# One core, decay attention feeding two expert layers: VectorE pinned in the first block, later attention twelve slots later

## The chip, the cores and the metric

One core of a Trainium2 chip runs the whole program once. The metric is the device time of that execution in microseconds (us). Engines: PE is TensorE, DVE VectorE, ACT ScalarE, POOL GpSimd, SP the queue that issues nearly all DMAs.

## What is computed

Cut from the reference (a batch of 4, 8 heads, 768 steps, head size 48):

```python
for t in range(S):                     # complex decay attention, one state per head
    new_re = ar * S_re - ai * S_im
    new_im = ar * S_im + ai * S_re
    S_re, S_im = new_re + k_t v_t, new_im
    y[t] = q_t @ S_re
x = y as (3072 tokens, 384)
h = x @ w_in                           # 384 to 2048
sp = log1p(exp(minimum(h, 20)))
x2 = (h * tanh(sp)) @ w_out            # 2048 to 384
out = (x2 @ w_a * (x2 @ w_b)) @ w2_out # 384 to 1536 to 384
```

## The kernel before

**Blocks, chunks, units.** The 768 steps are cut into six pieces of 128, and a chunk is one piece of one batch: 24 chunks, numbered 0 to 23, four of them (the four batches of one piece) make a block of 512 tokens. The first expert layer goes through six blocks, and in each through 16 units f of 128 columns of h. A unit computes `hps` (`moe1_h`, L544: nine matmuls, because f32 operands are split into a high and a low part), then on DVE and ACT the factor of the activation (`mish_factor`: the minimum of h on DVE at L550, then Exp, Square, Ln, Exp on ACT, each reading what the one before wrote), then on DVE the product with h (`mish_product`: L561 in the first block, which writes `gh`; L564 in the others), and two units later the matmuls of `moe1_x2` (L587) on that product. `hps` has two PSUM buffers in the first five blocks: the matmuls of unit f+2 wait until the product of unit f has read its `hps`. The second expert layer follows, 72 units of its own.

**Attention beside it.** The attention of chunks 0 to 3 is the lead-in, ahead of the first unit. Attention of chunks 4 to 23 runs beside the first layer in slots. A table (`early`, `late`) names the step and its slot relative to `slot_0(c)`; a new chunk starts every 8 slots. The steps that the prediction speaks of: `decay_1` to `decay_4` (Square on ACT; add on DVE, L250; Ln and Exp on ACT; DVE at L259, L265, L266, the first of which reads what Exp wrote), `angle` (Arctan on ACT), `carry` (DVE, L277), `split_ell` and `split_theta` (POOL L286, DVE L288 and L290, from chunk 8 on), the running sums on PE (`pl`, `pt`, L299), `reduce_angle` (DVE, L323 to L325), `trig` (two Sin on ACT), `rotate` (two DVE instructions of 128x768, L364, that read the sines), `transposes` (PE, copied out by ACT as `qT`, `kT`), `scores` (PE `psc`, DVE L399), `outer` (`pu`), `values` (`py`), `store_y2` (DVE `yl`, L440, then a DMA to memory) and `read_x` (the DMA that reads it back as `xh`, `xl`, the input of the next block's `hps`). ACT holds one table at a time: Exp and Ln need one, Sin and Arctan the other, and each change is an instruction of its own (L55).

**Weights.** In the first block each unit also takes a step of a loading pipeline (`do_w`): a 768 KB piece of the weights comes in as 64-bit words, three DVE instructions turn it into f32 (L166 to L168, tiles `wf` and `wout`), ACT copies the high part (`winh`, `wouth`) and POOL subtracts it (L178, `winl`, `woutl`).

**What sets the order.** The program is recorded in the order of the code, and a scheduler then chooses each engine's own order from its estimates, subject to the data. `in_order` and `behind` add artificial dependences: `in_order(first, engines)` makes each recorded instruction of an engine wait for the one recorded before it, so that the scheduler can't reorder them. Before, this is done for the lead-in alone. `run_to(n)` records the slots up to n; in a block with `base` to `want` slots, half of a unit's share comes ahead of the minimum of h (L550) and half ahead of the product. The first block runs to slot 46, where all of chunk 7 is done.

Of the kernel before, what the change touches and what calls it, by code (L numbers as in the profile page):

```python
# [21 lines left out]
def kernel(  # L22
# [27 lines left out]
    def act(**kw):  # L50


        name = TABLES.get(kw["func"])
        if name is not None and name != table["name"]:
            load = nc.scalar.preload_act_table_set(name)  # L55
            for y in table["ops"] + [table["last"]]:
                if y is not None:
                    follow(load, y)
            table.update(ops=[], last=load, name=name)
        x = nc.scalar.activation(**kw)  # L60
        if name is not None:
            follow(x, table["last"])
            table["ops"].append(x)

    B, H, S, D = q.shape
# [8 lines left out]
    NF = FF // P  # L74
# [125 lines left out]
    def w_cols(nm, f):  # L200
        return [w[:, :, f % 2 * P:(f % 2 + 1) * P] for w in weights[nm, f // 2]]
# [246 lines left out]
    def outer(c):  # L448
        if chunk(c)[0] == NC - 1:
            return  # L450
        kh, vt = st["kh", c], st["v", c]
        p = st["pu", c] = (ps_l if c < B else ps_a).tile([D2, H, D], F32, tag="pl" if c < B else "ps", name="pu")
        for h in range(H):
            nc.tensor.matmul(  # L454
                p[:, h, :], lhsT=kh[:, h].rearrange("p a d -> p (a d)"), rhs=vt[:, h * D:(h + 1) * D],
                start=True, stop=True,
            )

    def state(c):
        j, b = chunk(c)  # L460
        if j == NC - 1:
            return
        Wb = W[b][:D2, :H * D].rearrange("p (h d) -> p h d", d=D)
        us, g = st.pop(("pu", c)), st.pop(("g", c))
        if j:
            nc.vector.tensor_tensor(Wb, Wb, us, ALU.add)
            us = Wb
        (nc.gpsimd if us is Wb else nc.vector).tensor_tensor(Wb, us, g.to_broadcast([D2, H, D]), ALU.mult)
# [24 lines left out]
            nc.vector.tensor_tensor(xl, raw, xh.bitcast(F32), ALU.subtract)  # L493


    PERIOD = 8

    def slot_0(c):
        return PERIOD * (c - B)

    early = [
        (-5, load_a), (-1, decay_1), (0, decay_2), (0, decay_3), (1, tangent), (1, decay_4), (2, angle),
# [26 lines left out]
    def ready_slot(c):  # L529

        return slot_0(c) + late[-1][0] + 1
# [4 lines left out]
    def moe1_h(blk, f, pool):  # L536
        xh, xl = xh_t[blk], xl_t[blk]
        p = pool.tile([P, TN], F32, tag="ps" if pool is ps_a else "h", name="hps")
        hi, lo = w_cols("in", f)
        ops = []  # L540
        for kk in range(KM):
            ops += [(hi, xh, kk), (hi, xl, kk), (lo, xh, kk)]
        for i, (w, x, kk) in enumerate(ops):
            nc.tensor.matmul(p, lhsT=w[:, kk, :], rhs=x[:, kk, :], start=(i == 0), stop=(i == len(ops) - 1))  # L544
        return p

    def mish_factor(p):

        m = mp.tile([P, TN], F32, tag="m", name="m")
        nc.vector.tensor_scalar(m, p, 20.0, None, ALU.min)  # L550
        act(out=m, in_=m, func=AF.Exp)
        act(out=m, in_=m, func=AF.Square, bias=bias_one)
        act(out=m, in_=m, func=AF.Ln, scale=0.2, bias=bias_fifth)
        act(out=m, in_=m, func=AF.Exp, scale=-1.0)
        return m

    def mish_product(p, m, blk):

        if not blk:
            g = mp.tile([P, TN], F32R, tag="gh", name="gh").bitcast(F32)  # L560
            nc.vector.scalar_tensor_tensor(g, m, 2.5, p, ALU.subtract, ALU.mult)  # L561
            return [g]
        on_act = blk == NB - 1
        nc.vector.scalar_tensor_tensor(m, m, 2.5, p, ALU.subtract, ALU.mult)  # L564
        gh = mp.tile([P, TN], F32R, tag="gh", name="gh")
        gl = mp.tile([P, TN], F32R, tag="gl", name="gl")
        if on_act:
            act(out=gh, in_=m, func=AF.Copy)
        else:
            nc.vector.tensor_copy(gh, m)  # L570
        (nc.vector if on_act else nc.gpsimd).tensor_tensor(gl, m, gh.bitcast(F32), ALU.subtract)  # L571
        return gh, gl
# [157 lines left out]
    def run_to(n):  # L730
        while slot[0] < min(n, n_slots):
            attn_slot(slot[0])
            slot[0] += 1
# [23 lines left out]
    def do_w():  # L757
        next(weights1, None)
# [3 lines left out]
    def traced():  # L762
        return len(nc.cur_bb.bb.instructions)

    def in_order(first, engines):

        last = {}
        for x in nc.cur_bb.bb.instructions[first:]:
            if x.engine in engines:
                if x.engine in last:  # L770
                    tc.add_manual_dep(x, last[x.engine], no_sync, reason="lead")
                last[x.engine] = x.name
        return last

    def behind(first, last):
        for x in nc.cur_bb.bb.instructions[first:]:
            if x.engine in last:
                tc.add_manual_dep(x, last[x.engine], no_sync, reason="after the lead")
# [56 lines left out]
    E = mybir.EngineType  # L835
    first = traced()
    weights1 = lead_in()
    last, after_lead = in_order(first, (E.DVE, E.Activation, E.PE, E.Pool)), traced()
# [10 lines left out]
    def make_room():  # L849

        att.close()
        early.append(right.enter_context(tc.tile_pool(name="w2a", bufs=1, side="right")))
        spool.append(right.enter_context(tc.tile_pool(name="st2a", bufs=2, side="right")))
# [6 lines left out]
    ready, lag = {}, 2  # L860
    for ui in range(len(units) + lag):
        if ui == 3:
            behind(after_lead, last)
        if ui < len(units):
            blk, f = units[ui]
            if f == 0:
                base = slot[0]
                want = ends[blk + 1] if blk + 1 < NB else n_slots
                if blk == NB - 1:
                    make_room()  # L870
            p = moe1_h(blk, f, ps_a if blk == NB - 1 and f % 2 else ps_h)
            do_w()
            run_to(base + (want - base) * (2 * f + 1) // (2 * NF))
            m = mish_factor(p)
            if blk == 1 and f % 2 == 0:
                whole["out", f // 2][1]()
            if blk == NB - 1 and f % 5 != 4 or blk == NB - 2 and f >= NF - 2:
                next(prep, None)
        if ui == 1:
            for c in range(B):  # L880
                outer(c)
                state(c)
            tail.close()
            ps_x = w1.enter_context(tc.tile_pool(name="ps_x", bufs=1, space=PSUM))
            wps.append(allp.enter_context(tc.tile_pool(name="wp1", bufs=NF)))
        if ui >= lag:
            moe1_x2(*units[ui - lag], *ready.pop(ui - lag))
        if ui < len(units):
            run_to(base + (want - base) * (2 * f + 2) // (2 * NF))
            ready[ui] = mish_product(p, m, blk)  # L890

    w1.close()
    p2 = allp.enter_context(tc.tile_pool(name="p2", bufs=3))
# [210 lines left out]
```

## Time and profile before

| | us |
|---|---|
| three runs | 1108.72, 1111.19, 1113.58 (median 1111.19) |
| the profiled execution: its own time | 1108.67 |
| its span, first to last instruction | 1107.0 |
| PE busy | 1060.1 (96%) |
| DVE busy | 658.1 (59%) |
| ACT busy | 607.7 (55%) |
| POOL busy | 226.7 (20%) |

The profiled execution took 1108.67 us, of which 1107.0 are its span. The busy shares are averages over a lead-in, six blocks of the first layer and 72 units of the second; they say little of any one stage, so the stretches are asked for one at a time.

### The profile page before, as it was taken

Reading aid. Unit: us, or ns where it says so; the run is one execution under the profiler, and the core shown is the slowest. Engines: PE = TensorE matmul, PEld = TensorE weight load, DVE = VectorE, ACT = ScalarE, POOL = GpSimd, SP = SyncE. Lnnn points to the kernel's source line nnn. Section 1 sums busy time; section 2 is a strip of 40 time slices with the busy share of each in tenths; the row PEclk is TensorE's granted clock in tenths of the full one; section 3 lists DMA queues with packets and bytes.
Section 4 is the critical chain, followed back from the end, with each engine's and each line's share of the span. In section 5 each row is a group of like instructions: output and inputs, shape, how many; then the busy total and the mean of one; then the engine's idle time right before and its main releaser. Section 6 shows DMA issues by size and latency. Waiting matters only on the chain.

```text
span 1107.0 us, 15213 instructions
## 1 busy us (share of the span) xinstructions
PE 1060.1 (96%) x5740; PEld 882.8 (80%) x5740; DVE 658.1 (59%) x998; ACT 607.7 (55%) x962; POOL 226.7 (20%) x220
## 2 busy tenths in 40 slices
PE   3989989999999999999999999999999999999997
PEld 1856667888788788878877878888888888888886
DVE  4899995777777666777569998642322412322222
ACT  6669778888788787788757862221121222221211
POOL 2012163344333343343322122200000000000000
PEclk9999989999999999999999999999999999999999
DMA  9546754333444343334236366310010100100000
GB/s 201 107 123 172 191 142 96 95 65 72 96 85 86 81 94 65 65 74 98 65 91 200 123 196 215 104 57 1 21 38 1 43 15 1 43 1 1 29 1 31
DMA packets 203545, 90.87 MB, mean 82 GB/s; under 512 B 144781, under 2 KB 187850, under 8 KB 203466
## 3 DMA queue, kind: packets, MB, share of 16 engines
q1 hardware_dynamic: 203450, 89.82, 32.4%
q8 instruction: 47, 0.77, 0.3%
q14 instruction: 32, 0.26, 0.1%
q10 hardware_dynamic: 16, 0.01, 0.0%
HBM read 72.44 MB, written 17.36 MB: 81 GB/s over the span
## 4 chain that ended last, share of the span: by engine, by line
PE 73%; DVE 12%; ACT 8%; issue 4%; DMA 2%; POOL 0%; SPq 0%; ACTq 0%; DVEq 0%; POOLq 0%
PE ops L667 14%; PE psa L642 13%; PE psb L642 13%; PE hps L544 12%; PE x2ps L587 11%; ACT m L60 4%; PE psc L395 3%; PE py L419 2%; PE pu L454 2%; DVE m L550 2%; PE pqT L377 1%; PE pkT L377 1%; DVE m L564 1%; ACT s L60 1%; ACT L55 1%
## 5 line engine op out<-in xcount | busy, mean ns | idle before, releaser
L653 DVE TENSOR_TENSOR a_sb<-a_sb,psb 128x512 f32<-128x512 f32 x72 | 49.4, 686 | 224.5 <-PE psb L642 224.5
L60 ACT ACTIVATE m<-m 128x512 f32<-128x512 f32 x192 | 119.7, 627 | 81.3 <-DVE m L550 79.7
L60 ACT ACTIVATE ph<-a_sb 128x512 fp32r<-128x512 f32 x72 | 45.4, 631 | 156.9 <-DVE a_sb L653 156.9
L544 PE MATMUL hps<-xh,winh 128*128 128x512 f32 x288 | 120.3, 419 | 7.9 <-DVE gh L561 6.8
L60 ACT ACTIVATE a_sb<-psa 128x512 f32<-128x512 f32 x72 | 42.9, 596 | 153.9 <-PE psa L642 151.8
L571 POOL TENSOR_TENSOR gl<-m,gh 128x512 fp32r<-128x512 f32 x64 | 83.6, 1306 | 161.5 <-DVE gh L570 148.8
L544 PE MATMUL hps<-xl,winh 128*128 128x512 f32 x288 | 114.3, 397 | 0.4 <-DMA xl<-yt_dl 0.3
L544 PE MATMUL hps<-xh,winl 128*128 128x512 f32 x288 | 113.8, 395 | 0.0
L667 PE MATMUL ops<-woh,ph 128*128 128x384 f32 x288 | 97.3, 338 | 0.0
L667 PE MATMUL ops<-woh,pl 128*128 128x384 f32 x288 | 97.2, 338 | 0.0
L587 PE MATMUL x2ps<-gl,wouth 128*128 128x512 f32 x240 | 94.8, 395 | 2.2 <-DVE gl L571 1.1
L667 PE MATMUL ops<-wol,ph 128*128 128x384 f32 x288 | 96.8, 336 | 0.0
L587 PE MATMUL x2ps<-gh,wouth 128*128 128x512 f32 x240 | 93.9, 404 | 2.3 <-ACT gh L60 1.9
L587 PE MATMUL x2ps<-gh,woutl 128*128 128x512 f32 x240 | 93.8, 391 | 0.0
L642 PE MATMUL psa<-xh,wal 128*128 128x512 f32 x216 | 85.3, 395 | 0.0
L642 PE MATMUL psa<-xl,wah 128*128 128x512 f32 x216 | 85.2, 394 | 0.0
L642 PE MATMUL psa<-xh,wah 128*128 128x512 f32 x216 | 84.4, 391 | 0.0
L642 PE MATMUL psb<-xh,wbh 128*128 128x512 f32 x216 | 84.3, 390 | 0.0
L642 PE MATMUL psb<-xh,wbl 128*128 128x512 f32 x216 | 84.3, 390 | 0.0
L642 PE MATMUL psb<-xl,wbh 128*128 128x512 f32 x216 | 84.2, 390 | 0.0
L564 DVE SCALAR_TENSOR_TENSOR m<-m,hps 128x512 f32<-128x512 f32 x80 | 54.5, 683 | 37.1 <-ACT m L60 37.0
L655 DVE TENSOR_TENSOR pl<-a_sb,ph 128x512 fp32r<-128x512 f32 x72 | 52.3, 726 | 38.9 <-ACT ph L60 38.9
(143 smaller groups left out, 2349.0 us busy)
## 6 DMA issues: line engine op xcount, KB each, us to landing
wraw<-in_moe_w_out_dram SPq DMA_DIRECT2D x14, 768.0 KB
wraw<-in_moe_w_in_dram SPq DMA_DIRECT2D x8, 768.0 KB
a<-in_a_re_dram SPq DMA_DIRECT2D x24, 192.0 KB
a<-in_a_im_dram SPq DMA_DIRECT2D x24, 192.0 KB
q<-in_q_dram SPq DMA_DIRECT2D x24, 192.0 KB
k<-in_k_dram SPq DMA_DIRECT2D x24, 192.0 KB
v<-in_v_dram SPq DMA_DIRECT2D x24, 192.0 KB
wraw<-in_moe_w_a_dram SPq DMA_DIRECT2D x6, 768.0 KB
```

The lines of the kernel that those rows point to most:

```text
L60: x = nc.scalar.activation(**kw)
L377: nc.tensor.transpose(p[:, i, :], src[:, hf * HH + i].rearrange("p a d -> p (a d)"), ident)
L395: nc.tensor.matmul(p[:, i, :], lhsT=st["kT", c, hf][:, i, :], rhs=st["qT", c, hf][:, i, :], start=True, stop=True)
L419: nc.tensor.matmul(p[par * 64:(par + 1) * 64, i, :], lhsT=w[:, col:col + 64], rhs=x[:, first + par, :], start=(n == 0), stop=(n == len(ter ...
L544: nc.tensor.matmul(p, lhsT=w[:, kk, :], rhs=x[:, kk, :], start=(i == 0), stop=(i == len(ops) - 1))
L564: nc.vector.scalar_tensor_tensor(m, m, 2.5, p, ALU.subtract, ALU.mult)
L571: (nc.vector if on_act else nc.gpsimd).tensor_tensor(gl, m, gh.bitcast(F32), ALU.subtract)
L587: nc.tensor.matmul(x2ps[m], lhsT=w[:, ms], rhs=x, start=(f == 0 and i == 0), stop=(f == NF - 1 and i == len(terms) - 1),)
L642: nc.tensor.matmul(p, lhsT=w[:, kk, :], rhs=x[:, kk, :], start=(i == 0), stop=(i == len(ops) - 1))
L653: nc.vector.tensor_tensor(a_sb, a_sb, pb, ALU.mult)
L655: nc.vector.tensor_tensor(lo, a_sb, hi.bitcast(F32), ALU.subtract)
L667: nc.tensor.matmul(ops_t[t], lhsT=x[:, tsl], rhs=w, start=(f == 0 and i == 0), stop=(f == NF2 - 1 and i == 2),)
```

## The change

Three things. In the first block the minimum of h is recorded right after a unit's `hps`, ahead of the weight step and the slots, and the product ahead of `moe1_x2` and of the second half of the slots; the other blocks keep their code. When the 16 units of the first block are recorded, DVE is pinned to the recorded order from the lead-in's end to that point. And `slot_0` of chunks 8 to 23 is 12 slots higher, so that the second block has 44 slots (46 to 90) instead of 32 and the blocks after it 32 as before.

```diff
-    PERIOD = 8
+    PERIOD, REST = 8, 12
 
     def slot_0(c):
-        return PERIOD * (c - B)
+
+        return PERIOD * (c - B) + (REST if c >= 2 * B else 0)
...
     for ui in range(len(units) + lag):
         if ui == 3:
             behind(after_lead, last)
+        if ui == NF:
+            in_order(after_lead, (E.DVE,))
...
             p = moe1_h(blk, f, ps_a if blk == NB - 1 and f % 2 else ps_h)
+            if not blk:
+                m = mish_factor(p)
             do_w()
             run_to(base + (want - base) * (2 * f + 1) // (2 * NF))
-            m = mish_factor(p)
+            if blk:
+                m = mish_factor(p)
+            else:
+                ready[ui] = mish_product(p, m, blk)
...
             run_to(base + (want - base) * (2 * f + 2) // (2 * NF))
-            ready[ui] = mish_product(p, m, blk)
+            if blk:
+                ready[ui] = mish_product(p, m, blk)
```

DVE in the first block, before, from the minimum of unit 2 on (numbers tell the buffers apart; `m_793` is unit 3):

```order
L550 TENSOR_SCALAR m_748<-hps_724 128x512
L250 TENSOR_TENSOR s_746<-s_746 128x384
L166 TENSOR_SCALAR wf32_780<-wraw_649 128x768
L550 TENSOR_SCALAR m_793<-hps_770 128x512
L167 SCALAR_TENSOR_TENSOR wf32_780<-wraw_649,wf32_780 128x768
L168 SCALAR_TENSOR_TENSOR wf32_780<-wraw_649,wf32_780 128x768
L259 TENSOR_TENSOR a_630<-a_630,r_762 128x384
L265 TENSOR_SCALAR s_746<-s_746 128x384
L561 SCALAR_TENSOR_TENSOR gh_768<-m_748,hps_724 128x512
```

The same place now, unit 3 whole (`m_780` to the minimum of unit 4, `m_832`), behind the end of unit 2:

```order
L562 SCALAR_TENSOR_TENSOR gh_754<-m_734,hps_724 128x512
L250 TENSOR_TENSOR s_752<-s_752 128x384
L259 TENSOR_TENSOR a_631<-a_631,r_764 128x384
L265 TENSOR_SCALAR s_752<-s_752 128x384
L266 SCALAR_TENSOR_TENSOR size_767<-r_764,s_752 128x384
L551 TENSOR_SCALAR m_780<-hps_770 128x512
L166 TENSOR_SCALAR wf32_786<-wraw_655 128x768
L167 SCALAR_TENSOR_TENSOR wf32_786<-wraw_655,wf32_786 128x768
L168 SCALAR_TENSOR_TENSOR wf32_786<-wraw_655,wf32_786 128x768
L562 SCALAR_TENSOR_TENSOR gh_799<-m_780,hps_770 128x512
L364 TENSOR_TENSOR qh_807<-q_661,a_202 128x768
L364 TENSOR_TENSOR kh_809<-k_663,a_202 128x768
```

Every unit now reads minimum, three decode instructions, product, attention. Work that stood between L250 and its reader L259 stands elsewhere, and no minimum comes ahead of the product before it.

ACT beside it now, from the last step of unit 3's factor to the first of unit 4's:

```order
L60 ACTIVATE m_780<-m_780 128x512
L55 ACT_TABLE_LOAD
L60 ACTIVATE a_202<-a_202 128x384
L60 ACTIVATE a_202<-a_202,bias_hpi_68 128x384
L60 ACTIVATE a_631<-a_631 128x384
L55 ACT_TABLE_LOAD
L60 ACTIVATE winh3_839<-wf32_786 128x768
L60 ACTIVATE qT0_128<-pqT_849 96x512
L60 ACTIVATE kT_860<-pkT_855 96x512
L60 ACTIVATE m_832<-m_832 128x512
```

The pair of sines `a_202` that L364 reads stands behind unit 3's factor and a table change, and unit 4's factor behind two changes, three activations and three copies.

PE at the seam of the first two blocks, before (`gh_1600` is unit 14's product, `hps_1676` the first unit of the second block):

```order
L377 MATMUL pkT_1662<-ident_61,kh_1622 96x128 x4
L587 MATMUL x2ps0_754<-gh_1600,wout7_1412 128x512
L587 MATMUL x2ps1_756<-gh_1600,wout7_1412 128x512
L299 MATMUL pt_1669<-sh_1645,csum_r_63 128x384
L299 MATMUL pt_1669<-sl_1646,csum_r_63 128x384
L377 MATMUL pqT_1686<-ident_61,qh_1620 96x128 x4
L377 MATMUL pkT_1692<-ident_61,kh_1622 96x128 x4
L587 MATMUL x2ps2_758<-gh_1600,wout7_1412 128x512
L544 MATMUL hps_1676<-xh_1023,winh0_275 128x512
```

The sums and transposes there belong to chunks 8 and 9, and the second block's first unit needs the product of unit 14.

The same place now (`hps_1542` is unit 15, `hps_1580` and `hps_1618` are the first two of the second block, `gh_1565` is unit 15's product):

```order
L545 MATMUL hps_1542<-xh_455,winl7_1402 128x512
L588 MATMUL x2ps0_756<-gh_1470,wout6_1262 128x512
L588 MATMUL x2ps1_758<-gh_1470,wout6_1262 128x512
L588 MATMUL x2ps2_760<-gh_1470,wout6_1262 128x512
L588 MATMUL x2ps0_756<-gh_1515,wout7_1405 128x512
L588 MATMUL x2ps1_758<-gh_1515,wout7_1405 128x512
L588 MATMUL x2ps2_760<-gh_1515,wout7_1405 128x512
L588 MATMUL x2ps0_756<-gh_1565,wout7_1405 128x512
L545 MATMUL hps_1580<-xh_1024,winh0_275 128x512
L545 MATMUL hps_1618<-xh_1024,winh0_275 128x512
```

The attention work is gone from the seam, and the second block's first matmul now stands behind the product of unit 15, the last of the first block.

## Rows read from the trace of the kernel before

**Rows 1.** The page, busy time and share of the span by engine.

```profile
PE 1060.1 (96%) x5740; PEld 882.8 (80%) x5740; DVE 658.1 (59%) x998; ACT 607.7 (55%) x962; POOL 226.7 (20%) x220
```

**Rows 2.** Stretches, first and second block: busy us (count) per engine, clock, DMA.

```profile
58.40:187.80 129.40, 119.12 (x648) 83.37 (x647) 113.67 (x163) 102.09 (x158) 40.80 (x30) 0.96 0.60 154
187.80:284.70 96.90, 96.39 (x607) 79.87 (x605) 69.71 (x110) 78.08 (x122) 37.01 (x39) 1.00 0.36 77
```

**Rows 3.** Timeline, DVE, first block: start us, length us, what, [idle before].

```profile
59.21 0.55 DVE L166 TENSOR_SCALAR wout<-wraw 128x768 uint32<-128x768 uint32 x1
59.68 0.95 DVE L167 SCALAR_TENSOR_TENSOR wf<-wraw,wf 128x768 uint32<-128x768 uint32 x1
62.28 0.95 DVE L168 SCALAR_TENSOR_TENSOR wout<-wraw,wout 128x768 uint32<-128x768 uint32 x1
63.15 0.69 DVE L550 TENSOR_SCALAR m<-hps 128x512 f32<-128x512 f32 x1
...
148.04 0.68 DVE L550 TENSOR_SCALAR m<-hps 128x512 f32<-128x512 f32 x1
...
181.56 0.68 DVE L550 TENSOR_SCALAR m<-hps 128x512 f32<-128x512 f32 x1
```

**Rows 4.** Stretch from the first unit to unit 11's minimum, columns as in 2.

```profile
58.40:148.00 89.60, 82.22 (x445) 57.60 (x444) 83.55 (x120) 70.08 (x107) 24.02 (x16) 0.98 0.62 166
```

**Rows 5.** Timeline, DVE and ACT, unit 6's minimum, factor and product.

```profile
105.20 0.68 DVE L550 TENSOR_SCALAR m<-hps 128x512 f32<-128x512 f32 x1
105.92 0.63 ACT L60 ACTIVATE m<-m 128x512 f32<-128x512 f32 x1 [0.91 <-DVE m L550]
...
108.09 0.63 ACT L60 ACTIVATE m<-m 128x512 f32<-128x512 f32 x1
...
108.76 0.69 DVE L561 SCALAR_TENSOR_TENSOR gh<-m,hps 128x512 f32<-128x512 f32 x1
```

**Rows 6.** Timeline, ACT, a change of tables and back.

```profile
123.32 0.63 ACT L60 ACTIVATE m<-m 128x512 f32<-128x512 f32 x1
123.97 1.28 ACT L55 ACT_TABLE_LOAD   x1
125.26 0.52 ACT L60 ACTIVATE a<-a 128x384 f32<-128x384 f32 x1
...
127.20 1.28 ACT L55 ACT_TABLE_LOAD   x1
```

**Rows 7.** Timeline, DVE and ACT, the sum of decay_2 and its Ln and Exp.

```profile
118.03 0.55 DVE L250 TENSOR_TENSOR s<-s 128x384 f32<-128x384 f32 x1
118.62 0.85 ACT L60 ACTIVATE s<-s 128x768 f32<-128x768 f32 x1 [2.03 <-DVE s L250]
119.50 0.85 ACT L60 ACTIVATE r<-s 128x768 f32<-128x768 f32 x1
```

**Rows 8.** Timeline, POOL and DVE, weight split and decode side by side.

```profile
63.75 1.80 DVE L277 SCALAR_TENSOR_TENSOR a<-size,a 1x384 f32<-1x384 f32 x1
...
142.97 6.83 POOL L178 TENSOR_TENSOR woutl<-wout,wouth 128x768 fp32r<-128x768 f32 x3 [0.34 <-ACT wouth L60]
...
145.67 2.44 DVE L167 SCALAR_TENSOR_TENSOR wout<-wraw,wout 128x768 uint32<-128x768 uint32 x1
```

**Rows 9.** Timeline, DVE and PE, the store of y and the third block's first units.

```profile
279.27 0.68 DVE L440 TENSOR_TENSOR yl<-py,yh 128x512 fp32r<-128x512 f32 x1
...
286.29 0.50 PE L544 MATMUL hps<-xl,winh 128*128 128x512 f32 x1 [0.29 <-DMA xl<-yt_dl]
```

**Rows 10.** Timeline, PE, first and third unit of the second block.

```profile
187.75 0.79 PE L544 MATMUL hps<-xh,winh 128*128 128x512 f32 x1
188.39 0.40 PE L544 MATMUL hps<-xl,winh 128*128 128x512 f32 x1
188.62 0.39 PE L544 MATMUL hps<-xh,winl 128*128 128x512 f32 x1
...
200.03 0.50 PE L544 MATMUL hps<-xh,winh 128*128 128x512 f32 x1
```

## The prediction

> **What bounds the kernel now.** The page comes first: PE is busy for 96% of the span, DVE and ACT for little over half [rows 1]. So PE's work is the floor, and only stretches in which PE is kept waiting can give time back. The stretches by block come next, cut at the first matmul of each block's first unit. In the first block PE is idle for 129.4 - 119.1 = 10.3 us and its granted clock is 0.96; in the second it is idle for 0.5 us at 1.00 [rows 2]. The 4% of clock over 129 us are about 5 us more. All that can be recovered is therefore some 15 us, in the first block; elsewhere PE has no slack. There DVE is the bound, busy 113.7 of 129.4 us, with ACT at 102.1; in the second block DVE has 69.7 and ACT 78.1 of 96.9 [rows 2]. The timelines then give the pieces from which the new order is priced.
>
> **How I price it.** I follow DVE down the printed order of the first block. An instruction starts when the one before it lets go (start to start 0.47 for a 768-column L166, 0.87 for L167 and L168, 0.60 for a 128x512 that reads PSUM [rows 3, 8]), or later, when what it reads is late. Times below are of the profiled execution, which took 1108.67, 2.5 under the median of the runs.
>
> **Part 1, work moved out of the first block.** Compared with the order before, 17 DVE instructions of chunks 8 to 10 leave it: two L364 (I take 0.87 each, as for L167 of the same width), two short ones (0.3) and thirteen of the length of L250, 0.55 less the 0.08 by which such instructions overlap [rows 3, 7]. That is 1.7 + 0.6 + 6.1 = 8.4 us off the engine that bounds the block, nearly all behind unit 9. They come back in the second block, where they are covered as long as PE stays the bound there.
>
> **Part 2, the fixed order.** Each unit is now minimum, three decode instructions, product, attention. Four waits follow from it, none of which the order before had so often:
> - The product behind the decode. With ACT free, product starts 108.76 - 105.20 = 3.56 after minimum [rows 5]; minimum and decode fill 0.60 + 2.21 = 2.81. Idle 0.75, in units 3 and 6 (elsewhere other work or a longer wait covers it): 1.5 us.
> - The product behind a change of tables. After the factor of units 0, 3, 6 and 9 ACT loads a table, does its angles and loads back: 123.97 to the end of the second load at 128.48, 4.5 us with a copy (yh) in it, 4.1 without [rows 6]. Then come a weight copy and copies for the transposes, and the next factor mixed with three more copies, which I put at 3.85 instead of 2.8. DVE idles 2.8, 1.1, 2.5 and 2.2 us in units 1, 4, 7, 10: 8.6 us.
> - rotate behind its sines. They start only after the unit's factor and a load, 1.29 for the load and 2 x 0.45, the 0.52 of such an activation less its overlap: 2.2 after it [rows 6], against 0.6 of product and at most 0.6 of yl: 1.6, 1.1 and 2.5 us in units 3, 6, 9: 5.2 us.
> - L259 behind Ln and Exp, which end 2.3 after L250 starts [rows 7], with one or two short instructions between: 1.8, 1.1, 1.2 us in units 2, 5, 8: 4.1 us.
>
> The sum is 19.4 us of DVE idle up to unit 11's minimum. Before, DVE idled 89.6 - 83.55 = 6.0 there [rows 4]. So the fixed order costs 13.4. Against it stand two gains. Weight decode that runs beside POOL's weight split is stretched, 2.44 against 0.95 [rows 3, 8]: by some 10 us in nine stretched instructions up to unit 11, of which the first and the last are in [rows 8], and by some 2.5 in the new order, where the split mostly falls beside waits or PSUM readers, which keep their 0.68: 7.5 off. And of part 1 some 4 us lie ahead of unit 11, and unit 0's minimum comes ahead of one decode, at 61.5 instead of 63.15 [rows 3]. Together 13.4 - 7.5 - 4 - 1.6 = +0.3: unit 11's minimum at 148 to 149, where it was at 148.04 [rows 3]. I take 148.9.
>
> What an idle DVE costs PE is bounded below by nothing (if PE has other matmuls ready) and above by all of it; I take all, because PE needs product f for unit f+2 and has two buffers.
>
> **Part 3, the end of the block.** From unit 11 to unit 15 it took 181.56 - 148.04 = 33.5 us [rows 3]. Now: unit 11 takes 0.6 + 2.2 + 0.6 + 0.6 + 0.5 and 0.2 idle = 4.7; unit 12, with rotate, two steps of another decode and 3 us of stretch, 10.1; units 13 and 14 wait for ACT, which copies the wouth there, 6.1 and 5.6. That makes 26.5, so unit 15's minimum stands at 175.4, 6 us earlier. The store of chunk 7's y is recorded behind that minimum and has to go to memory and back: 286.29 - 279.27 = 7.0 from yl to the first matmul that needs all of it [rows 9]. With yl at 176, the second block is under way at 182.5 to 183, against 187.75 [rows 10]: 5 us earlier.
>
> **Part 4, the second block.** It takes over what left. At its start ACT has decay and a table change ahead of unit 0's factor, and PE has little to do beside: the product of unit 0 ends at about 190, and unit 2 begins there, 9.8 earlier than the 200.03 before [rows 10]. But one chunk's matmuls that were done by then are still to come. Their size: 96.9 us of block less 16 x 18 matmuls at 0.23 [rows 2, 10], over four chunks, 7.7 us. That leaves 2.1. The next three units wait for ACT once more (two loads and a mixed factor), 1.3, and the rest of the block, with three slots per unit where two were, I give 1 us more of small waits than before. Remaining: 0 or slightly under. The blocks behind it keep their 32 slots and their order, and the second layer is untouched: nothing there.
>
> **The sum:** first block -5, second block +5, thus 1108.7 in the profiled frame, and 1109.5 as the time I give, between that and the median of 1111.2. The gain of part 1 is real, but is spent on the waits of part 2 and at the seam.
>
> **A rule against the change.** The order now has two table loads more. In the trace a load follows the last activation by 0.02 us, takes 1.28, and the next activation starts 0.01 after it [rows 6]. The Trainium skill (ScalarE: Activation LUTs, What ACT_TABLE_LOAD costs) gives 1283 ns for the load and another 1380 ns of drain, 2.66 us for each switch. The trace agrees on the first and shows no such drain; were it hidden somewhere, each of the four pairs ahead of a product would cost 2.8 more, and the kernel would come to 1120. By the rows it is nothing; I leave it 3 in 100.
>
> **Rivals.**
> - PE takes its slack back (28 in 100). If PE has other matmuls ready during half of the waits of part 2, and the stretched decode vanishes, the first block goes to near its own work: 129.4 - 10.3 - 5 = 114. Half of that 15 us kept makes 1101. For it: DVE's load in the block falls by 8.4, and PE idled only 7.4 of 89.6 us up to unit 11 [rows 4], though DVE was full. Against it: two buffers of h, and every product now waits for ACT.
> - ACT bounds the second block, and the kernel is slower (17 in 100). ACT's 78.1 us less 16 factors of 2.8 leave 33, 8.3 a chunk [rows 2, 5]; with 1.5 chunks more ACT has 91 us of work. PE has 96.4 + 7 = 103. It decides if ACT idles as much as before, 96.9 - 78.1 = 19: then the block takes 110 instead of 103, and the kernel 1116. Against it: that idle time was mostly waiting for PE's own pace.
> - The drain above: 1120 (3 in 100).
> - That the order isn't as described is excluded by the printed order; its effect isn't.
>
> **Chances.** A measurement of this kernel can tell about 0.5%, 5.5 us, from no change. My forecast and its neighbourhood of 5.5 us have 52 in 100, the first rival 28, the two slower ones 20. The range reaches to both rivals: 1100 to 1118.
>
> **What would show it.** Right: DVE's busy time in the first block near 100 us, with idle time ended by ACT m (product), ACT a (rotate) and ACT r (L259) of some 15 to 20 us in place of 6; stretched L166 to L168 fewer; unit 11's minimum at 147 to 151; the second block's first hps at 180 to 185, its third unit near 190; ACT above 88 us there. Wrong: PE idle in the first block under 5 us with the second block at its old pace (first rival), or a second block over 108 us (second rival).

## The result, and the profile after

The changed kernel takes 1121.08 us (median of 6 runs, 1118.51 to 1124.81), the kernel before 1111.03 (6 runs): ratio 1.0097, with a 95% interval of 1.0075 to 1.0118. It is slower by some 10 us, and 1121.08 lies outside the predicted range. The profiled execution took 1119.39 us, its span is 1117.6: 10.6 more than before.

Stretches of the kernel after: first block up to unit 11's minimum and from there to its end, then second and third block (us, then busy us and count for each engine, the granted clock behind POOL's):

```profile
58.20:154.60 96.40, 85.47 (x434) 58.11 (x433) 77.79 (x114) 65.31 (x99) 13.89 (x11) 0.93 0.54 144
154.60:190.80 36.20, 34.09 (x193) 22.17 (x192) 24.41 (x30) 27.26 (x41) 20.02 (x13) 1.00 0.58 142
...
190.80:300.95 110.15, 105.00 (x659) 87.16 (x658) 83.44 (x135) 94.33 (x148) 44.32 (x46) 0.98 0.38 80
300.95:395.40 94.45, 94.10 (x598) 79.00 (x596) 67.62 (x109) 77.16 (x121) 37.66 (x40) 1.00 0.39 81
```

Two stretches of the kernel before that [rows 2, 4] do not have, the end of the first block and the third block:

```profile
148.00:187.75 39.75, 36.85 (x203) 25.73 (x203) 30.10 (x44) 31.96 (x51) 16.79 (x15) 0.91 0.55 128
...
284.70:384.60 99.90, 98.74 (x624) 82.68 (x624) 71.34 (x113) 80.41 (x127) 38.34 (x41) 1.00 0.39 82
```

Over both of its stretches the first block is 132.6 us long (129.4 before, [rows 2]) although 22 matmuls have left it. The second is 13.2 longer and the third 5.5 shorter; behind them nothing changes. Over the three blocks that is 11.0 us. PE's idle time explains 6.6 of it: 2.8 more in the first block, 4.6 more in the second, 0.8 less in the third. The other 4.4 us are more busy time for the same matmuls: the granted clock is 0.95 in the first block (0.96 before) and 0.98 in the second (1.00 before).

What DVE waited for in the first block (line it waited at, what it waited for, us in total, times, longest), after:

```profile
DVE gh L562 <- ACT m L60: 14.6, 9, 3.5
DVE qh L364 <- ACT a L60: 4.9, 3, 2.1
DVE a L259 <- ACT r L60: 3.9, 3, 1.8
DVE W L468 <- PE pu L454: 2.2, 1, 2.2
DVE W L466 <- PE py L419: 1.9, 1, 1.9
```

Before, the first of these was 1.3 us and the next two together 0.2. Where it hurts most is unit 9. DVE's timeline after (start us, length us):

```profile
137.28 0.68 DVE L551 TENSOR_SCALAR m<-hps 128x512 f32<-128x512 f32 x1
137.88 0.55 DVE L166 TENSOR_SCALAR wf<-wraw 128x768 uint32<-128x768 uint32 x1
138.46 0.96 DVE L167 SCALAR_TENSOR_TENSOR wf<-wraw,wf 128x768 uint32<-128x768 uint32 x1
139.46 0.96 DVE L168 SCALAR_TENSOR_TENSOR wf<-wraw,wf 128x768 uint32<-128x768 uint32 x1
140.33 0.68 DVE L440 TENSOR_TENSOR yl<-py,yh 128x512 fp32r<-128x512 f32 x1
143.16 0.96 DVE L364 TENSOR_TENSOR qh<-q,a 128x768 f32<-128x768 f32 x1 [2.14 <-ACT a L60]
144.03 0.95 DVE L364 TENSOR_TENSOR kh<-k,a 128x768 f32<-128x768 f32 x1
144.90 0.68 DVE L562 SCALAR_TENSOR_TENSOR gh<-m,hps 128x512 f32<-128x512 f32 x1
```

The factor is ready at 140.8, but the product stands behind rotate, rotate behind its sines, and these behind a load of ACT's table. PE has run out of other work by then (its timeline):

```profile
144.17 1.09 PE L377 MATMUL pqT<-ident,qh 128*96 128x128 f32 x4 [4.06 <-DVE qh L364]
```

A measure used below: a unit's **loss** is its length, from its first `hps` to the next unit's, less its matmuls at the spacing that they have where nothing disturbs them; it is worked out from PE's timeline. In unit 10 (the wait above lies between its first `hps` and unit 11's) it is 7.0 us, the largest of the block; before it was 2.2.

### The profile page after: what moved, and what is told of

Its sections match the earlier page's. It is cut to its first block, busy times and chain, and to the rows that moved or that the text cites. A ratio compares the mean times of both kernels' runs of the same rounds, so it can differ in the third digit from the quotient of the medians.

```text
span 1117.6 us, 15210 instructions
## 1 busy us (share of the span) xinstructions
PE 1063.8 (95%) x5740; PEld 883.0 (79%) x5740; DVE 654.0 (59%) x998; ACT 611.4 (55%) x964; POOL 226.8 (20%) x220
## 4 chain that ended last, share of the span: by engine, by line
PE 64%; ACT 14%; DVE 13%; issue 7%; DMA 1%; POOL 0%; SPq 0%; ACTq 0%; POOLq 0%; DVEq 0%
PE ops L668 13%; PE psa L643 13%; PE psb L643 13%; PE hps L545 9%; PE x2ps L588 8%; ACT m L60 7%; DVE m L551 2%; ACT L55 2%; PE psc L395 2%; PE py L419 2%; DVE kh L364 1%; ACT s L60 1%; ACT a L60 1%; PE pu L454 1%; DVE m L565 1%
## 5 line engine op out<-in xcount | busy, mean ns | idle before, releaser
L668 PE MATMUL ops<-wol,ph 128*128 128x384 f32 x288 | 96.7, 336 | 0.0
L551 DVE TENSOR_SCALAR m<-hps 128x512 f32<-128x512 f32 x96 | 65.4, 682 | 19.0 <-PE hps L545 16.3
```

Source lines behind the costliest of these rows:

```text
L668: nc.tensor.matmul(ops_t[t], lhsT=x[:, tsl], rhs=w, start=(f == 0 and i == 0), stop=(f == NF2 - 1 and i == 2),)
```

## The experiments

The three parts of the change can be made apart: A, VectorE held to the recorded order in the first block; B, the early minimum and product; C, the twelve slots. "Held" below means with A, "free" without it. Theory 1 is that A costs, because DVE stands behind waits for ACT. Theory 2 is that C costs, because the second block gets too full.

### The parts alone and in pairs

Each kernel is the one before with the named parts of the diff:

```diff
+    PERIOD, REST = 8, 12                      # C
+        if ui == NF:                          # A
+            in_order(after_lead, (E.DVE,))
+            if not blk:                       # B
+                m = mish_factor(p)
+                ready[ui] = mish_product(p, m, blk)
```

C alone: 

> Only the move back by 12 slots (the first block keeps the order it had). Theory 1, the fixed VectorE order is what costs: without it the moved work relieves the first block, the second block starts at 181 to 184 us instead of 187.75 and takes 100 to 103 us, and the kernel is at 1106 to 1111 us. Theory 2, the twelve slots cost, because the second block gets half as much attention again and ScalarE is loaded there: the second block takes 107 to 111 us, and the kernel is at 1115 to 1121 us.

A and B: 

> The fixed VectorE order and the early minimum in the first block, all chunks in their old slots. Theory 1 (the fixed order costs): the first block keeps all of its work and gets some 17 us of VectorE waits ahead of unit 11's minimum, so the block takes 136 to 142 us where it took 129.4, the second block stays at 97, and the kernel is at 1117 to 1125 us. Theory 2 (the slots cost): the first block takes 128 to 133 us and the kernel is at 1107 to 1113 us.

B and C: 

> The new order of recording in the first block and the twelve slots, but VectorE not held to that order. Theory 1 (the fixed order costs): VectorE can take other work while a product, a rotate or L259 waits for ScalarE; its idle time up to unit 11's minimum falls from 18.6 to under 9 us, and the kernel is at 1107 to 1113 us. Theory 2 (the slots cost): the second block still takes 107 to 111 us and the kernel stays at 1115 to 1121 us.

A and C: 

> VectorE held to the order in which the kernel before records its work (product after the unit's attention, minimum after the matmuls of the unit), with the twelve slots. Theory 1 (the fixed order costs by its waits for ScalarE): the product is recorded late, so it no longer waits for its factor, but a unit's matmuls wait for the late product; rotate and L259 still wait; the kernel is at 1113 to 1120 us. Theory 2 (the slots cost): the second block takes 107 to 111 us and the kernel is at 1115 to 1121 us, whatever the first block does.

B alone: 

> Only the early minimum and the product recorded ahead of the unit's second matmuls, no held order, all chunks in their old slots. If the early minimum is what gains (the kernel with both, without the held order, was at 1107.3, the twelve slots alone at 1111.2): 1105 to 1109 us. If it gains only together with the twelve slots: 1110 to 1113 us.

| parts | median us | ratio to before (95%) | first block us | second block us |
|---|---|---|---|---|
| B | 1106.94 | 0.9946 (0.9928 to 0.9965) | 127.0 | 95.8 |
| C | 1111.16 | 1.0005 (0.9987 to 1.0022) | 122.6 | 110.0 |
| B, C | 1107.30 | 0.9960 (0.9943 to 0.9977) | 118.6 | 109.3 |
| A, B | 1126.98 | 1.0157 (1.0127 to 1.0187) | 147.4 | 96.4 |
| A, C | 1135.83 | 1.0220 (1.0191 to 1.0249) | 141.4 | 114.7 |
| A, B, C | 1121.08 | 1.0097 (1.0075 to 1.0118) | 132.6 | 110.1 |

A costs 14 us beside B and C, 20 beside B alone, and 25 beside C alone. B alone gains 4.6. C gives nothing where the order is free: the first block gets 6.7 us shorter and the second and third together 7.6 longer. Only where the order is held is C worth 6 us. Theory 2 was right on the second block's length and wrong on what it costs. Two expectations missed: A with C is worse than either theory said, and A with B went 2 us above what theory 1 gave it, with a first block of 147 us instead of 136 to 142. B, alone or with C, is faster than both kernels.

### Which units of the held order

```diff
-        if ui == NF:
+        if ui == 12:                          # pin_head: units 0 to 11
             in_order(after_lead, (E.DVE,))
```

> The changed kernel with VectorE held to the recorded order in units 0 to 11 only. Theory 3 (the waits of the first twelve units are paid there, but what keeps them from being won back is the end of the block, where the held order lets no work of chunk 8 and no weight decode ahead of the products): the first block ends 4 to 8 us earlier than 190.8, chunk 8's first L250 stands before unit 15's minimum, the kernel is at 1111 to 1116 us. Rival (the whole cost lies in the waits up to unit 11): unit 11's minimum near 154, and the kernel at 1119 to 1122 us.

The other kernel takes the mark from which the order holds at unit 12: 

> The changed kernel with VectorE held to the recorded order in units 12 to 15 only. Theory 3 (the end of the block costs 6 to 8 of the 13.8 us): unit 11's minimum at 140 to 143, as without any held order, but the second block loses PE time at its start: 1111 to 1116 us. Rival (the whole cost lies in the waits up to unit 11): 1106 to 1109 us.

The first took 1126.05 us (1.0121, 1.0097 to 1.0145), the second 1114.31 (1.0033, 1.0014 to 1.0052). The second came as theory 3 said, the first as neither did: holding units 0 to 11 costs some 19 us against B and C alone, and holding units 12 to 15 costs 7. That the first costs more than holding all 16 is not shown: the two intervals overlap, and its second block starts at 192.6, only 1.8 us behind the changed kernel's 190.8. The stretch up to unit 11's minimum where the units to there are held:

```profile
58.20:154.90 96.70, 86.24 (x437) 59.23 (x436) 77.74 (x114) 65.30 (x99) 13.87 (x11) 0.93 0.55 144
```

The same stretch and the rest of the block where only units 12 to 15 are held:

```profile
58.50:140.70 82.20, 78.89 (x439) 55.23 (x439) 76.12 (x117) 66.93 (x103) 18.43 (x12) 1.00 0.64 171
140.70:183.30 42.60, 34.89 (x186) 22.96 (x185) 26.41 (x27) 24.49 (x37) 19.42 (x12) 0.92 0.47 118
```

And where none is held (B and C):

```profile
58.20:141.30 83.10, 80.25 (x443) 55.88 (x442) 78.61 (x120) 66.96 (x103) 20.57 (x14) 1.00 0.64 169
141.30:176.80 35.50, 32.94 (x181) 21.58 (x180) 22.19 (x30) 26.96 (x40) 17.10 (x12) 0.95 0.57 145
```

DVE does about the same work in all three, 76 to 79 us. Held, it takes 96.7 us for it, of which 19.0 are idle; free, 83.1, of which 4.5 are idle. So the waits up to unit 11 do cost about their size: 14.5 us more idle time, 13.6 us more in all. The second stretch shows something that I had not expected: when unit 11 comes early and the end is held, the end takes 42.6 us, where the changed kernel needed 36.2.

### Which wait

Free the three waiting instructions from the held order, or free the decode, or take ACT's table changes away (one line of each edit):

```diff
+                free.append((a, traced()))    # product, L259, rotate; or do_w
+            if i >= first and x.engine in engines and not (len(engines) == 1 and any(a <= i < z for a, z in free)):
-        act(out=w[:, 0], in_=t[:, 0], func=AF.Sin, scale=SIN_SCALE)
+        act(out=w[:, 0], in_=t[:, 0], func=AF.Square, scale=SIN_SCALE)
```

> The changed kernel, VectorE held to the recorded order in the first block except for the three kinds of instruction that wait for ScalarE there (product, rotate, L259), which are placed as before. Theory 1 (VectorE standing behind these waits is what the fixed order costs): their 14.6 us of idle time ahead of unit 11's minimum and the 8.7 in units 13 to 15 mostly go, the first block takes 119 to 124 us, the kernel 1107 to 1112 us. Rival (the fixed order of the rest costs, minimum and decode in fixed turns, whoever waits): under 4 us of the 13.8 come back, 1117 to 1121 us.

It took 1117.72 us (1.0048, 1.0032 to 1.0063). The first block came to 122.3 us, as theory 1 had it, but the second took 117.4, and 7 of the 10 us were lost again; the kernel's time came out at the rival's end. DVE's timeline at the seam shows how it begins (L260 and L567 are L259 and the product here):

```profile
176.92 1.39 DVE L250 TENSOR_TENSOR s<-s 128x384 f32<-128x384 f32 x1
180.56 2.40 DVE L260 TENSOR_TENSOR a<-a,r 128x384 f32<-128x384 f32 x1 [2.25 <-ACT r L60]
...
183.15 0.67 DVE L567 SCALAR_TENSOR_TENSOR gh<-m,hps 128x512 f32<-128x512 f32 x1
```

Unit 15's product is placed behind an L260 of the next chunk that first waits and then is stretched, and the second block's first matmuls wait 2.7 us for it. With B and C alone the same L250 ran at 161.8, two units earlier. That is 2.7 of the 7 us; the rest was not followed.

> The changed kernel, VectorE held to the recorded order except for the weight decode, which may run ahead. Theory 1 (idle time behind waits for ScalarE): decode has no need of ScalarE, so where it is free it fills some of these waits, but the waits themselves remain and the rest is queued behind them: some third to two thirds of the 13.8 us come back, 1111 to 1117 us. Rival (the waits cost PE nothing, the order of the decode beside GpSimd's weight split does): decode runs into the split as it likes, nothing comes back, 1119 to 1124 us.

It took 1130.99 us (1.0166, 1.0141 to 1.0190): both expectations missed. Unit 3's minimum already stood at 91.7 instead of 87.3, and in the first block DVE waited 23.3 us for factors instead of 14.6. To fill an engine is not to shorten its chain; what in the free decode makes the chain longer was not followed further.

> The changed kernel with Square in place of Sin and Arctan, so that ScalarE never changes its table (the angles are then wrong numbers; as many activations as before). In the fixed order a pair of loads of 1.28 us each stands ahead of the factor of units 1, 4, 7, 10 and one of them ahead of rotate. Theory 1: VectorE's idle time ahead of unit 11's minimum falls from 18.6 to 8 to 12 us, and the kernel comes to 1108 to 1114 us. Rival (the loads are hidden beside ScalarE's other idle time): 1117 to 1121 us.

> The same replacement where VectorE is not held to an order (early minimum and twelve slots alone, 1107.3 us with its tables). Theory 1: other VectorE work covers the loads in the first block, so at most 3 us come back there; if ScalarE's load is what makes PE idle for 4.5 us in the second block, 2 to 4 us come back there: 1102 to 1107 us. Rival (the second block's idle time comes from the chain of hand-overs of the attention, not from ScalarE's load): second block unchanged at 109 us, kernel 1105 to 1108 us.

They took 1118.41 us (1.0050, 1.0032 to 1.0069) and 1099.52 (0.9892, 0.9869 to 0.9914). In the held order DVE's idle time up to unit 11's minimum fell from 18.6 to 13.8 us and that minimum came at 147.6 (1.3 us of this were gained in the lead-in already), but the rest of the block then took 42.6 us, as with only units 12 to 15 held:

```profile
147.60:190.20 42.60, 34.72 (x191) 22.79 (x189) 30.19 (x30) 24.18 (x38) 20.86 (x13) 0.92 0.53 127
```

Without the held order ACT has 16.6 us less to do in the second block, and PE's idle time there goes from 4.5 to 3.8 us only:

```profile
176.00:283.40 107.40, 103.56 (x653) 85.69 (x654) 80.32 (x126) 74.62 (x129) 45.92 (x47) 1.00 0.39 82
```

So ACT's load explains little of PE's idle time in a fuller second block. The gain in the free order is 7.8 us by the medians, 9.0 in the profiled executions. It lies in the lead-in (1.3) and in the second to the fifth block (0.7 to 3.1 in each); the first has nothing of it. Theory 1 missed in both: held, idle time fell less than it said and the time was the rival's, and free, the kernel was faster than either expectation.

### What holds the end of the block

Two reliefs of the held order (free_waits and nosin_abc) had brought unit 11's minimum from 154.6 to 149.6 and 147.6, and the kernel got only 3 us faster by each. The last runs ask why: take two waits out of the order, move the product, take away POOL's weight split, beside which DVE instructions are stretched, by letting POOL write zeros (memset), and do two at once.

```diff
+            r += B < c < 2 * B and fn in (tangent, decay_4, rotate)        # late_rot
-                ready[ui] = mish_product(p, m, blk)                        # late_prod: recorded at the unit's end
-            nc.gpsimd.tensor_tensor(lo, f[0], hi.bitcast(F32), ALU.subtract)
+            nc.gpsimd.memset(lo.bitcast(F32), 0.0)                         # memset, first layer only
```

> The changed kernel, with L259 (and the two short instructions behind it) and rotate of chunks 5 to 7 recorded half a unit to one unit later, so that in the held order L259 stands behind the next unit's decode and rotate behind the product. Theory 1 (VectorE's idle time behind these waits is the cost): of their 8.8 us ahead of unit 11's minimum at most 3 remain, PE's 7.0 us of loss in unit 10 (rotate ahead of product) falls to under 3, unit 11's minimum comes at 146 to 150 instead of 154.6, and the kernel is at 1111 to 1116 us. Rival (the order waits for ScalarE at the next place instead): unit 11's minimum at 152 to 155, the kernel at 1118 to 1122 us.

> The changed kernel, with the factor early but the product recorded behind the unit's second matmuls and attention, as in the kernel before. Theory 1 read simply (the product's own idle time of 5.8 us ahead of unit 11 and 8.7 behind it is the cost): it falls to under 4 us in all and the kernel is at 1110 to 1116 us. Rival (a late product costs more than a waiting one, because PE's next unit but one needs its buffer): PE waits longer for products, the first block takes 135 to 142 us and the kernel 1122 to 1132 us.

> The changed kernel, with the low part of the first layer's weights set to zero by GpSimd, in place of GpSimd's subtraction that makes it. If the stretched VectorE instructions lie on the path of the held order: the 5.7 us up to unit 11 and some 4 behind it go, and the kernel is at 1110 to 1115 us. If the idle time just grows by as much: 1117 to 1121 us.

> The same replacement without the held order (early minimum and twelve slots, 1107.3 us). If the stretch lies on the path there too: the 5.2 us up to unit 11 go, unit 11's minimum comes at 135 to 138 instead of 141.3, and the kernel is at 1101 to 1104 us. If PE has other work to cover it: 1105 to 1108 us.

> Both edits at once: L259 and rotate recorded later, and zeros in place of GpSimd's subtraction for the first layer's weights (their low part is left out), in the held order. If two limits take turns (waits for ScalarE up to unit 11, stretched decode and rotate ahead of products in units 12 and 13): unit 11's minimum near 150, unit 12's product at 161 to 164 instead of 169 to 173, the second block starts at 180 to 185, and the kernel is at 1110 to 1115 us. If a third thing holds the end of the block: the second block starts at 188 to 193, the kernel is at 1118 to 1123 us.

| kernel | median us | ratio to before (95%) | unit 11's minimum | second block starts |
|---|---|---|---|---|
| A, B, C | 1121.08 | 1.0097 (1.0075 to 1.0118) | 154.6 | 190.8 |
| late_rot | 1123.40 | 1.0101 (1.0073 to 1.0129) | 150.2 | 192.8 |
| late_prod | 1126.68 | 1.0121 (1.0090 to 1.0153) | 152.5 | 193.0 |
| memset_abc | 1120.46 | 1.0072 (1.0043 to 1.0100) | 154.6 | 189.7 |
| late_rot_ms | 1113.14 | 1.0009 (0.9989 to 1.0029) | 148.0 | 183.2 |
| memset_bc | 1103.27 | 0.9921 (0.9893 to 0.9949) | 138.7 | 172.0 |

The zeros in the held order are the cleanest reading of the study. Its row up to unit 11's minimum, to be put beside the first row of the kernel after:

```profile
58.20:154.60 96.40, 86.39 (x432) 59.04 (x431) 72.34 (x115) 65.40 (x99) 6.13 (x11) 0.91 0.54 145
```

DVE is busy for 72.3 us instead of 77.8, and the stretch is as long as before, to a tenth of a microsecond: what the instructions lose in length, the waits gain. It holds turn by turn too: the minima of units 2 to 7 and 9 to 11 come within 0.2 us of those in the kernel after. In the free order the same edit gives 5.0 us of the first block (113.6 for 118.6), and the kernel is 4.0 faster. The time of memset_abc understates its first two blocks, which are 2.2 us shorter together: in its profiled execution the fourth block took 102.5 us instead of 99.3, with PE waiting 2.5 us for DMAs, and why isn't known.

late_rot does what it should up to unit 11: of 8.8 us behind L259 and rotate 1.7 are left, and unit 10's loss falls from 7.0 to 1.4. But the kernel came out above both expectations. Unit 12's product comes 12.5 us behind its minimum (timelines of DVE and POOL in late_rot; L564 is the product):

```profile
156.72 0.68 DVE L553 TENSOR_SCALAR m<-hps 128x512 f32<-128x512 f32 x1
...
162.22 2.15 DVE L166 TENSOR_SCALAR wf<-wraw 128x768 uint32<-128x768 uint32 x1 [1.11 <-POOL winl L178]
164.40 2.45 DVE L167 SCALAR_TENSOR_TENSOR wf<-wraw,wf 128x768 uint32<-128x768 uint32 x1
166.88 2.44 DVE L168 SCALAR_TENSOR_TENSOR wf<-wraw,wf 128x768 uint32<-128x768 uint32 x1
169.24 0.67 DVE L564 SCALAR_TENSOR_TENSOR gh<-m,hps 128x512 f32<-128x512 f32 x1
...
162.14 13.83 POOL L178 TENSOR_TENSOR woutl<-wout,wouth 128x768 fp32r<-128x768 f32 x6
```

Six of POOL's splits run as one piece of 13.8 us, and the decode beside them, which the held order puts ahead of the product, is stretched from 2.5 to 7.0 us. With both edits the product follows sooner (DVE in late_rot_ms; L567 is the product):

```profile
154.61 0.68 DVE L556 TENSOR_SCALAR m<-hps 128x512 f32<-128x512 f32 x1
...
161.41 0.68 DVE L567 SCALAR_TENSOR_TENSOR gh<-m,hps 128x512 f32<-128x512 f32 x1
```

So the two limits (waits for ACT up to unit 11, stretched decode and rotate ahead of the products of units 12 and 13) take turns: each relief alone gives at most 1 us, both together 8, and the expectation came about, with unit 11's minimum 2 us earlier than said. What is left against the free order is 6 us (10 against the free order with zeros). late_prod came to the rival's time, but not by its way: in the first block PE waits only 0.8 us for products, and 7.8 for what rotate writes, which DVE now reaches later. Its first two blocks are 3.1 us longer than the changed kernel's; the fourth is 4.2 longer, and nothing here ties that to the edit.

### Two more

```diff
-    PERIOD, REST = 8, 12
+    PERIOD, REST = 8, 6                       # bc_rest6, no held order
-            if not blk:
+            if blk < NB - 1:                  # b_all, no held order, old slots
```

> Early minimum, no held order, and 6 slots in place of 12. If PE's 4.5 us of idle time in the second block come from its density of attention (44 slots over 16 units where 32 were), 38 slots leave 1 to 2.5 us of them, while the first block keeps over half of the relief: 1103 to 1107 us. If idle time does not follow the density, or the first block needs all twelve: 1107 to 1110 us.

> Early minimum and early product in all blocks but the last, no held order, old slots. If the gain of 4.6 us comes from a VectorE that is the bound, only the first block has that, and the kernel stays at 1105 to 1109 us. If PE's small losses in the later blocks (4 to 5 us each) wait for products too, 1100 to 1104 us.

Six slots gave 1108.16 us (0.9965, 0.9950 to 0.9980), no better than none (B alone) or twelve. PE idled 4.0 us in a second block of 104.2, where it idles 0.3 with none (B alone) and 4.5 with twelve, so its idle time there does not grow in step with the slots; which hand-over makes it stays open. The early product in all blocks gave 1116.84 (1.0041, 1.0025 to 1.0058): outside both expectations. Where PE is the bound, an early product costs: the third, fourth and fifth block take 102.4, 102.3 and 95.7 us, where B alone has 100.1, 99.6 and 90.6. PE now waits for rotate, in those three blocks too, where with B alone it doesn't (b_all, whole kernel):

```profile
PE pqT L377 <- DVE qh L364: 10.2, 16, 0.9
```

## Why the prediction was wrong

By its own steps:

- **The bound** was read rightly in part. In the free order the first block went to 118.6 us, and with zeros to 113.6; the prediction gave 114 for a block near its own work. But 6.7 us of this are the work that C moved out, and it came back behind the block. And without table changes some 8 us were gained outside the first block, where the prediction saw no slack.
- **Part 1** held roughly: DVE has 20 instructions less in the first block (17 were counted), and its busy time fell by 11.4 us, to 102.2 ("near 100").
- **Part 2, the waits**, held in sum: 18.6 us of idle time up to unit 11's minimum, 19.4 predicted. Rotate (4.9 for 5.2) and L259 (3.9 for 4.1) were close; the product waited 5.8 us instead of 10.1, and 4.0 of other waits, 2.2 of them behind PE's `pu`, were not foreseen.
- **The step that failed is the line "Together 13.4 - 7.5 - 4 - 1.6 = +0.3".** Measured, the stretch up to unit 11's minimum grew by 6.8 us, from 89.6 to 96.4. The waits are 12.6 of it, near the 13.4. The two credits on busy time, 7.5 and 4, brought 5.8 together: 4.5 of the stretched time went (10.2 before, 5.7 after, by the mean lengths of the lines), and of part 1 one L250 alone had stood ahead of unit 11's minimum. The decode, priced at 2.21, takes 2.45 in unit 9 above. The last credit gave nothing: unit 0's minimum came at 61.7, as said, but the decode that it passed still had to be done, and unit 2's minimum was at 79.0, 1.6 later than before. Unit 11's minimum came at 154.6 instead of 148.9.

  Right credits would not have saved the line, because it adds busy time and idle time of one engine as if they did not know of each other. The run with zeros shows that they do. There DVE's busy time is 72.3 us, 11.2 less than before and so what the line assumes, but the waits are 24.1, 18.0 more than before instead of 13.4, and unit 11's minimum is at 154.6 again. So it was partly luck that the waits in the kernel after came near their price: the stretched instructions filled 5.5 us of them. DVE's waits up to unit 11's minimum, the product after, then with zeros the product and the waits for `pu` (here by "issue", for nothing that the profile shows) and `py`:

```profile
DVE gh L562 <- ACT m L60: 5.8, 6, 2.4
...
DVE gh L565 <- ACT m L60: 9.2, 7, 2.8
...
DVE W L471 <- issue: 2.9, 1, 2.9
DVE W L469 <- PE py L422: 1.5, 2, 1.0
```

  With zeros the product waits nearly as long as priced (10.1); what the prediction put at nothing are the 4.4 us in front of W. My reading is that in a fixed order with a wait in each turn the turn's length is that of the chain through it (minimum, factor on ACT, as in unit 9 above a table change, the sines and rotate, then product and next minimum), and shortening what stands beside the chain gives nothing; the lengths along the chain were not added up for each turn.
- **Part 3** was short by 4.3 us: 30.8 from unit 11 to unit 15, not 26.5. Unit 11 took 7.3 for 4.7 (DVE, held, waited 2.4 for PE), and unit 12 took 11.8 for 10.1, with rotate and decode stretched beside POOL's split:

```profile
165.59 2.01 DVE L364 TENSOR_TENSOR qh<-q,a 128x768 f32<-128x768 f32 x1
167.53 2.56 DVE L364 TENSOR_TENSOR kh<-k,a 128x768 f32<-128x768 f32 x1
170.01 2.17 DVE L166 TENSOR_SCALAR wf<-wraw 128x768 uint32<-128x768 uint32 x1
```

  Units 13 and 14 (6.3 and 5.4 for 6.1 and 5.6) were right. The second block began at 190.8, 4.8 us after its `yl`, instead of 182.5 to 183.
- **Part 4** was short by 2.7 us over the second and third block together (204.6, where the sum has 201.9). The third unit was at 200.1, 9.3 behind the first, for 7.3 predicted. That the third block would give work to the second was not seen.
- So some 8 us of the miss lie in the first block, and 2.7 in the second and third.

**The rivals.** The first (PE takes its slack back, 1101) is what the free order does in part: 1107.3. The second gave the second block's length, 110, but its reason fell: with 16.6 us less on ACT, in the free order, PE idled nearly as long. Part of that length is work of the third block, the rest PE's 5 us of idle time. The third, a drain at each change of tables, gave 1120; that the measured time lies near it is chance. In the kernel after, ACT's timeline has the load right behind an activation and the next activation right behind the load:

```profile
140.17 0.63 ACT L60 ACTIVATE m<-m 128x512 f32<-128x512 f32 x1
140.80 1.28 ACT L55 ACT_TABLE_LOAD   x1
142.09 0.52 ACT L60 ACTIVATE a<-a 128x384 f32<-128x384 f32 x1
```

The Trainium skill (ScalarE: Activation LUTs, What ACT_TABLE_LOAD costs) states 1283 ns for the load and some 1380 ns of drain for each switch. The trace agrees on the load, 1.28 us; it shows no such drain, only 0.01 us between the load and the next activation.

## What to carry to other kernels

Before an engine is held to an order, follow the longest chain through one turn of that order and take its length as the time; work beside the chain is not part of the sum, and making it shorter only lengthens the waits. Where two limits take turns, an edit that removes one shows nothing: try both at once before one is given up. Finally, change one part at a time: here the early minimum alone gains 4.6 us, the twelve slots nothing, and the held order loses three times what the minimum gains.

## What the runs showed of the hardware that I had not expected

- DVE instructions of 128x768 in SBUF that took 0.96 us alone took 2.0 to 2.6 beside POOL's subtraction of 128x768 (above), while products that read PSUM kept their 0.67 to 0.69. Writing zeros in place of the subtraction took 5.0 us off the first block where DVE's order is free, and 1.2 where it is held. Beside two pieces of zeros an L166, 0.55 us alone, took 1.52 (memset_abc, DVE and POOL):

```profile
163.11 1.52 DVE L166 TENSOR_SCALAR wout<-wraw 128x768 uint32<-128x768 uint32 x1
...
162.80 0.73 POOL L179 MEMSET woutl<- 128x768 f32 x1
163.48 0.73 POOL L179 MEMSET winl<- 128x768 f32 x1
```

- Taking all table changes away gained 7.8 us in the free order (nosin_bc against B and C). The fourth block got 2.3 us shorter, though PE had been busy there for 98.8 of 100.1 us. What shortens that block was not followed.
- TensorE's granted clock stayed at 1.00 up to unit 11 in the free order, where PE idled 2.9 of 83.1 us, and was 0.93 in the held one, where it idled 10.9 of 96.4. PE was busy for 85.5 us there instead of 80.3, with nine matmuls less: a wait cost more than its own length.
